# Instruction order taken from the text in place of a scheduler's, with alpha loaded a chunk sooner and the folds and first splits moved

## Chip, cores and metric

One core of one Trainium2 chip. The metric is the device time of one execution in microseconds (us); lower is better. Every time below is in us unless something else is said. Fast runs alone are compared: an execution over 1.5% above the fastest of the same kernel counts as slow.

## The reference, cut to what matters

```python
# q, k, v, alpha: (4, 8, 768, 48) fp32
for t in range(768):                                   # gated linear recurrence
    state = alpha[:, :, t, :, None] * state + einsum('bhd,bhe->bhde', k[:, :, t], v[:, :, t])
    y[:, :, t] = einsum('bhd,bhde->bhe', q[:, :, t], state)
x = y.transpose(0, 2, 1, 3).reshape(3072, 384)         # fp32
out = (((x @ w1) * (x @ w2)) @ w3) @ w_out             # weights float64: 384x1024, 1024x1024, 1024x384
```

## The kernel before

The work falls into three phases, and TensorE (matmul) has to do with all of them:

1. **Recurrence**: 24 chunks of 128 tokens. Per chunk: the running sum of log alpha (`decays`), transposes of q and k, scores, masked attention (`attend`). Its x goes to device memory and comes back transposed, three chunks at a time, as a "token group"; the first gates of groups 0 to 4 are worked in between, from chunk 5, 9, 13, 17 and 21 on.
2. **Gate phase**: the remaining products `x @ w1`, `x @ w2`, each split into three fp32r products (`exact`), and between them eight **folds**, which multiply a row block of w3 into w_out.
3. **Output phase**: 24 projections.

Beside that, VectorE and ScalarE convert float64 weights, bit by bit, into fp32 (`to_fp32`). Each conversion is cut into steps by `yield`, and the text says where a step stands. Before the change a scheduler then moved instructions; the text was only its input.

```python
def to_fp32(dst, *srcs):
    ...                                                     # load raw
    yield
    nc.scalar.activation(rest, low, AF.Copy, scale=2.0 ** -52)                              # L189
    nc.vector.tensor_scalar(top, high, ...)                                                # L190
    nc.vector.tensor_scalar(power, high, 20, 0x7FF, ...)       # exponent, shifted          # L193
    nc.scalar.activation(power, power, AF.Relu, scale=2.0 ** 23, bias=rebias)              # L194
    yield
    nc.vector.scalar_tensor_tensor(mant, top, 2.0 ** -20, rest, ...)                       # L196
    nc.vector.scalar_tensor_tensor(power, high, 0x80000000, power, ...)                    # L197
    nc.vector.tensor_mul(to, mant, power.bitcast(FP32))                                    # L199
    yield
...
def attend(n):
    ...
    for i in range(2):
        nc.scalar.copy(st["x", n][:, :, i], y[i])                                          # L352
    ...
    for half in range(2):
        nc.scalar.dma_start(out=to[half, ...], in_=x[ds(DP * half, D)])    # x to memory    # L358

def load_x(g, queue=nc.sync):
    st["xT", g] = xp.tile([C, KM, TG], FP32, tag="xT", name="xT")
    queue.dma_start(out=st["xT", g], in_=xd[g]...)                                         # L363

def split_x(g, i):
    ...
    nc.scalar.activation(t[:, 0], x, ...)                                                  # L369
    nc.vector.tensor_sub(t[:, 1], x, ...)                                                  # L370
    nc.vector.scalar_tensor_tensor(t[:, 2], ...)                                           # L371

def exact(to, w, x, scale):
    p1, p2 = two of eight PSUM banks
    ... matmuls into p1                                                                    # L380
    nc.scalar.activation(t, p1, AF.Copy, scale=...)            # frees p1                   # L382
    ... matmuls into p2                                                                    # L384
    nc.vector.scalar_tensor_tensor(to, p2, -scale, t, ...)     # frees p2                   # L385
...
for n in range(N):                                             # recurrence
    load_v(n + AHEAD - 1); load_a(n + 5); load_kq(n + AHEAD)
    scores(n)
    if n - 1 in begin:                                         # begin = 4, 8, 12, 16, 20
        split_x(g, 0); fill.extend(gates)
    ...
    early = n < 7
    convert(1, 2 if n == 0 else 3)                             # one step of a conversion
    run(n - 1 not in begin)                                    # half a gate
    advance(n); outer(n)
    if early:
        convert(1)
    transposed(n + 1); decayed(n + 2); logs(n + 4)
    if n in begin:
        load_x(begin[n][0], nc.scalar)
    convert(early and n > 2)
    run(1)
    decays(n + 3); load_ends(n + 2)
    convert(early or n % 3 == 0)
    attend(n)
    run(n - 1 in begin)
```

## Time and profile before

| | before |
|---|---|
| median | 508.95 (508.44 to 510.96, 3 runs) |
| span of the profiled run | 506.3 |
| TensorE busy | 476.6 (94%) |
| first gate starts, last `attend` starts, first projection starts | 56.32, 212.7, 402.68 |

The windows view cuts the span at those three points. Columns: window, its length, then for TensorE, its weight loads, VectorE, ScalarE and GpSimd the busy time with the number of instructions, then the granted TensorE clock, the share of the DMA engines and GB/s.

```profile
0.00:56.30 56.30, 35.95 (x392) 26.11 (x392) 34.37 (x64) 31.01 (x63) 4.65 (x25) 0.91 1.04 198
56.30:212.70 156.40, 150.65 (x1584) 128.20 (x1584) 121.36 (x209) 93.77 (x204) 11.54 (x18) 0.97 0.83 179
212.70:402.70 190.00, 190.00 (x1023) 172.56 (x1020) 146.81 (x277) 90.57 (x166) 0.00 (x0) 1.00 0.39 126
```

Subtract busy from length to read it: TensorE idles for 20.4 before the first gate, 5.8 in the rest of the recurrence, and for nothing in the gate phase, where it has full clock and no gap in 190. VectorE (146.8 of 190) and ScalarE (90.6) have room there. That is a phase in which an order of instructions can only lose.

### The profile page before, as it was taken

To read this page: it belongs to the slowest core of one execution; us is meant where nothing else is said; L and a number is where in the kernel's file an instruction comes from. 1 tells how busy PE (TensorE), PEld (TensorE's weight loads), DVE (VectorE), ACT (ScalarE), POOL (GpSimd) and SP (SyncE) were. 2 spreads that over 40 slices of the span, in tenths; PEclk is the share of its full clock that TensorE was granted. 3 is DMA by queue.
4 is the path that set the end of the run, shared out by engine and by line. 5 is a ranking of instruction groups with operands and counts; after the bars stand their busy time and mean duration, and the time that the engine had idled before them with its cause. 6 is when DMAs were issued, how large, how long until landed. Compare 5 with 4: busy or idle time off the path is not lost.

```text
span 506.3 us, 9496 instructions
## 1 busy us (share of the span) xinstructions
PE 476.6 (94%) x3568; PEld 426.5 (84%) x3568; DVE 371.6 (73%) x620; ACT 250.7 (50%) x479; POOL 16.2 (3%) x43
## 2 busy tenths in 40 slices
PE   3878499999799999999999999999999999999997
PEld 2666388887688888899999988898889899999996
DVE  2777797999777667599999987877434597777771
ACT  3664664867487544365555545454223433333330
POOL 2000002200110000000000000000000000000000
PEclk9979699999899999999999999999999999999999
DMA  9989999999976733165665443321100776655511
GB/s 173 181 216 228 216 215 241 222 225 231 227 173 161 159 80 105 56 178 174 193 193 173 171 159 102 126 88 49 46 33 31 197 231 185 178 174 176 178 54 47
DMA packets 168734, 79.08 MB, mean 156 GB/s; under 512 B 112856, under 2 KB 162544, under 8 KB 168688
## 3 DMA queue, kind: packets, MB, share of 16 engines
q1 hardware_dynamic: 147184, 70.73, 55.3%
q10 hardware_dynamic: 21504, 7.75, 6.7%
q8 instruction: 28, 0.46, 0.4%
q14 instruction: 18, 0.15, 0.1%
HBM read 56.40 MB, written 22.06 MB: 155 GB/s over the span
## 4 chain that ended last, share of the span: by engine, by line
PE 73%; DVE 1%; issue 0%; DVEq 0%
PE bank L380 37%; PE bank L384 18%; PE bank L429 8%; PE bank L348 2%; PE bank L326 2%; PE bank L287 2%; PE bank L423 1%; PE bank L345 1%; PE bank L298 1%; PE bank L256 1%; DVE x L371 0%; DVE x L370 0%; DVE o L385 0%; DVEq L385 0%
## 5 line engine op out<-in xcount | busy, mean ns | idle before, releaser
L380 PE MATMUL bank<-x,w 128*128 128x384 f32 x768 | 162.8, 346 | 10.3 <-ACT x L369 8.0
L380 PEld LDWEIGHTS bank<-x,w 128*128 128x128 f32 x768 | 133.4, 189 | 16.6 <-ACT x L369 8.4
L382 ACT ACTIVATE t<-bank 128x384 f32<-128x384 f32 x152 | 74.4, 491 | 131.8 <-PE bank L380 103.0
L385 DVE SCALAR_TENSOR_TENSOR r<-bank,t 128x384 f32<-128x384 f32 x128 | 69.6, 554 | 49.6 <-ACT t L382 38.3
L384 PE MATMUL bank<-x,w 128*128 128x384 f32 x384 | 88.3, 337 | 1.3 <-DVE x L371 1.3
L384 PEld LDWEIGHTS bank<-x,w 128*128 128x128 f32 x384 | 68.6, 189 | 2.6 <-PE bank L380 1.4
L380 PE MATMUL bank<-w3o,ab 128*128 128x384 f32 x384 | 70.4, 334 | 0.0
L380 PEld LDWEIGHTS bank<-w3o,ab 128*128 128x128 f32 x384 | 66.9, 188 | 0.0
L429 PE MATMUL bank<-wo,w3T 128*128 128x384 f32 x128 | 42.6, 486 | 0.0
L384 PE MATMUL bank<-w3o,ab 128*128 128x384 f32 x192 | 37.2, 334 | 0.0
L429 PEld LDWEIGHTS bank<-wo,w3T 128*128 128x128 f32 x128 | 24.2, 189 | 14.9
L189 ACT ACTIVATE rest<-raw 128x512 f32<-128x512 uint32 (+1 forms) x36 | 23.3, 650 | 26.1 <-DMA raw<-in_moe_w_dram 23.6
L396 DVE TENSOR_TENSOR ab<-r 128x384 f32<-128x384 f32 x64 | 35.5, 555 | 0.9
L448 DVE TENSOR_TENSOR ab<-abl,ab 128x1024 fp32r<-128x1024 f32 x24 | 29.4, 1224 | 9.1 <-ACT ab L447 9.1
L447 ACT ACTIVATE ab<-abl 128x1024 fp32r<-128x1024 f32 x24 | 25.5, 1062 | 19.9 <-PE bank L384 18.8
L384 PEld LDWEIGHTS bank<-w3o,ab 128*128 128x128 f32 x192 | 33.6, 188 | 0.0
L329 DVE TENSOR_TENSOR ms<-bank,keep 128x512 int32<-128x512 int32 x48 | 31.1, 683 | 2.4 <-PE bank L326 2.4
L326 PE MATMUL bank<-qkT 48*128 48x128 f32 x384 | 28.8, 291 | 4.1 <-ACT qkT L288 4.1
L326 PEld LDWEIGHTS bank<-qkT 48*128 48x128 f32 x384 | 24.1, 193 | 9.6 <-ACT qkT L288 5.9
L287 PE MATMUL bank<-ident,qk 128*128 128x128 f32 x192 | 27.9, 291 | 3.9 <-DVE qk L268 3.9
L288 ACT COPY qkT<-bank 128x512 f32<-128x512 f32 x48 | 25.7, 586 | 10.2 <-PE bank L287 8.8
L268 DVE TENSOR_TENSOR qk<-kq,e 128x768 f32<-128x768 f32 x24 | 22.9, 954 | 10.2 <-ACT e L260 5.7
(65 smaller groups left out, 516.6 us busy)
## 6 DMA issues: line engine op xcount, KB each, us to landing
abd<-ab SPq DMA_DIRECT2D x64, 192.0 KB, 2.6
abl<-abd SPq DMA_DIRECT2D x24, 512.0 KB, 4.5
raw<-in_moe_w_dram SPq DMA_DIRECT2D x16, 512.0 KB, 4.4
raw<-in_moe_w_dram SPq DMA_DIRECT2D x24, 256.0 KB, 4.7
ac<-in_alpha_dram SPq DMA_DIRECT2D x24, 192.0 KB, 5.5
kq<-in_k_dram SPq DMA_DIRECT2D x24, 192.0 KB, 5.1
kq<-in_q_dram SPq DMA_DIRECT2D x24, 192.0 KB, 4.9
v<-in_v_dram SPq DMA_DIRECT2D x24, 192.0 KB, 4.7
```

The costliest lines, as they stand in the source:

```text
L287: nc.tensor.transpose(tp[:, ds(j * C, C)], qk[:, i, 2 * j:2 * j + 2, :], ident)
L288: nc.scalar.copy(qkT[:, i], tp.rearrange("p (j c) -> p j c", j=NP))
L326: nc.tensor.matmul(sc[i][:, j, :], qkT[r, 0, j, :], qkT[r, 1, j, :], start=True, stop=True)
L329: nc.vector.tensor_tensor(ms[:, i].bitcast(I32), sc[i].bitcast(I32), keep_bc, op=ALU.bitwise_and)
L380: nc.tensor.matmul(p1, w[part][i], x[part][i], start=(part == i == 0), stop=(part == 1 and i == n - 1))
L382: nc.scalar.activation(t, p1, AF.Copy, scale=(1.0 + 1.0 / P) * scale)
L384: nc.tensor.matmul(p2, w[2][i], x[2][i], start=(i == 0), stop=(i == n - 1))
L385: nc.vector.scalar_tensor_tensor(to, p2, -scale, t, op0=ALU.mult, op1=ALU.add)
L396: nc.vector.tensor_mul(ab, *r)
L429: nc.tensor.matmul(po, w3T[:, j, :], wo[:, j, :], start=(j == 0), stop=(j == KF - 1))
L447: nc.scalar.activation(t[:, 0], ab, AF.Copy, scale=1.0 - 2.0 ** -13)
L448: nc.vector.tensor_sub(t[:, 1], ab, t[:, 0].bitcast(FP32))
```

## The change

The intent is to take the order of instructions on every engine from the text (`manual_schedule`) and to move the text so that this order is a good one: alpha a chunk sooner, a fold in the loop ahead of the conversion of that gate, two first splits of the output phase between the last gates, and other rates of conversion. In full:

```diff
     nc = tc.nc
+    ctx.enter_context(tc.manual_schedule())
...
     def split_ab(n):
-        if n >= N:
+        if ("abl", n) not in st:
             return
...
     load_a(4)
+    load_a(5)
...
         load_v(n + AHEAD - 1)
-        load_a(n + 5)
+        load_a(n + 6)
...
         for _ in x:                       # one gate of the gate phase
             pass
-        owed += 2.7 if folds or folded else 1.2
-        convert(int(owed))
-        owed -= int(owed)
+        owed += 3.0 if folds or folded else 1.3
         if folded < KF:
             ...                           # one step of a fold
...
                 load_ab(n)
+            first = i
+        elif i - first in (1, 3):
+            split_ab(i - first >> 1)
+        convert(int(owed))
+        owed -= int(owed)
     store_ab()
-    split_ab(0)
-    split_ab(1)
+    for n in range(2):
+        split_ab(n)
```

## The prediction

> **What bounds the kernel now.** I read the page first (busy shares, then the 40 slices), then the waits of TensorE, then the timeline around each of its gaps. All times are microseconds.
>
> ```profile
> PE 476.6 (94%) x3568; PEld 426.5 (84%) x3568; DVE 371.6 (73%) x620; ACT 250.7 (50%) x479; POOL 16.2 (3%) x43
> PE   3878499999799999999999999999999999999997
> PEclk9979699999899999999999999999999999999999
> DMA  9989999999976733165665443321100776655511
> ```
>
> TensorE is busy for 94% of 506.3. Its gaps lie in the first eleven slices (to 139 us) and in the last. From 132 us to 502 the chain of waits is TensorE and nothing else, so no reordering can gain there; it can only open gaps. The whole idle time is 506.3 - 476.6 = 29.7, and some 10 of it is start (first alpha, first transposes) and end (last store). **At most about 20 us, 4%, is to be had**, all before 132 us. DMA is full up to slice 12 (150 us).
>
> TensorE's own waits say what the early gaps are:
>
> ```profile
> PE bank L380 <- ACT x L369: 8.0, 2, 6.3
> PE bank L253 <- ACT la L238: 5.6, 2, 4.4
> PE bank L326 <- ACT qkT L288: 4.1, 4, 2.8
> ...
> PE bank L380 <- DVE x L370: 2.3, 2, 1.5
> ```
>
> (total, times, longest.) The first gate of a token group waits for the split of its x (L369, L370, L371); one scores stage waits for the transposed q and k (L288).
>
> **What the change does to the order.** I compared the two programs engine by engine. TensorE's order is the same through the whole recurrence (chunks 0 to 23); only the folds move by a gate later on. What changes is ScalarE, VectorE and the queues: before, a scheduler put conversions and x loads early or late; after, each stands where the text has it. "TensorE: Matmul & The Clock Gate", section "Architectural detail", calls ScalarE and VectorE strict FIFO: so an instruction that waits for a transfer holds up all behind it. The trace agrees: the copies L288 below ran only after L189 had got its data at 30.16. So I go through the places where a text-order wait stands before something TensorE needs.
>
> **Part 1, first weight conversions.** Timeline of before, chunk 2 to 5:
>
> ```profile
> 30.16 0.69 ACT L189 ACTIVATE rest<-raw 128x512 f32<-128x512 uint32 x1 [2.58 <-DMA raw<-in_moe_w_dram]
> ...
> 32.31 1.05 ACT L288 COPY qkT<-bank 128x512 f32<-128x512 f32 x2
> ...
> 33.41 2.08 PE L326 MATMUL bank<-qkT 48*128 48x128 f32 x16 [2.79 <-ACT qkT L288]
> ...
> 42.46 0.39 ACTq L363 DMA_DIRECT2D xT<-xd  x1
> ...
> 55.10 1.17 ACT L369 ACTIVATE x<-xT 128x1152 fp32r<-128x1152 f32 x1
> ...
> 56.32 1.33 PE L380 MATMUL bank<-x,w 128*128 128x384 f32 x3 [6.27 <-ACT x L369]
> ```
>
> The second block of weights lands at 30.16. Before, its L189 stood behind the copies for scores of chunk 2 (those scores ran at 25.22). In text order it stands in front of them, and one alpha load (192 KB, about 0.9 us at the 220 GB/s of these slices) is now ahead of the block in the queue: landing about 31.1, then L190 and L193 (0.8), L194 (0.7), L288 twice (1.1): scores of chunk 2 at about 33.7 in place of 25.2. The chunk after an idle stretch took 7.8 in before (33.41 to 41.23), the next ones 5.3 of work, so chunk 5's transposes end at about 55 in place of 50.0. Half of the loss vanishes there, because before waits then anyway, to 56.32.
>
> What lets before wait is alpha of chunk 8 (L238 at 52.09, after 4.28 idle): **alpha a chunk sooner takes that wait away**. But it isn't the last obstacle any more: the load of x, which the scheduler had issued at 42.46, stands in the text behind chunk 8's logarithm, so it goes out at about 52. Its 576 KB need some 5.5 (the 512 KB loads of the page take 4.4 to 4.5 to land, with queues less full), then L369 1.2: first gate at about 59, +2.7, less the 0.8 that L370 no longer waits. **+1.9.**
>
> **Part 2, the other four x loads.** Groups 1 to 4 start after chunks 8, 12, 16 and 20. Before, group 2:
>
> ```profile
> 120.85 0.59 PE L256 MATMUL bank<-la,sums 128*128 128x384 f32 x2
> ...
> 126.31 1.17 ACT L369 ACTIVATE x<-xT 128x1152 fp32r<-128x1152 f32 x1
> ...
> 127.53 0.79 PE L380 MATMUL bank<-x,w 128*128 128x384 f32 x3 [1.70 <-ACT x L369]
> ```
>
> After, the load stands behind L242, which has one buffer and so waits for L256 of the chunk before it. So it goes out 0.6 after L256; lands about 5.3 later; L369 takes 1.2: 7.1. TensorE has, between L256 and the gate, attend 1.8, scores 1.1, outer 0.7, transposes 1.0: 4.5. **Gap 2.6, then 0.9 for L370 and 0.7 for L371 (1.35 each, less the 0.5 of three matmuls): 4.2.** The 3.8 of group 2 in before (1.70 + 1.51 + 0.57) was followed by a half clock from 131.2 to 135, which cost about 1.4 more. "TensorE: Matmul & The Clock Gate", "The HAM clock gate", says that about 3.4 us of idle window halve the clock and as much work restores it; the trace agrees roughly: 0.50 at 34 to 38, at 54 to 62 and at 132 to 135. So 5.6 a group. Group 1 had a 0.7 gap: +4.9. Group 2 had 5.2: +0.4. Group 3 had none: +5.6. Group 4 has no logarithm before its load, which goes out 2 us sooner: +3. **Sum +13.9.**
>
> "DMA: Bandwidth & Descriptors", "Issuing engines are not separate DMA queues", says that both queues share the 16 engines; so the ScalarE-issued load shares with the SyncE loads, which before kept the engines at 1.0 to 1.4 of their time there. For the change speaks that the weight loads are no longer hoisted: after chunk 7 one 512 KB block in three chunks, and no w_out block until the recurrence is over.
>
> **Part 3, folds.** One fold of before (timeline, 338 to 346):
>
> ```profile
> 338.95 5.32 PE L429 MATMUL bank<-wo,w3T 128*128 128x384 f32 x16
> ...
> 344.30 0.49 ACT L432 ACTIVATE w3o<-bank 128x384 fp32r<-128x384 f32 x1 [0.41 <-PE bank L429]
> 344.83 0.56 DVE L433 SCALAR_TENSOR_TENSOR w3o<-w3o,bank 128x384 fp32r<-128x384 f32 x1 [1.84 <-ACT w3o L432]
> ```
>
> After, VectorE's order in every second gate is L433, L434 of fold i, then L196, L197, L199 of the second half of w3 row i+1, and one gate later TensorE transposes that row. Counted from the end of L429 (344.27): L433 starts at +0.56, L434 ends at +1.6, then three operations that start 0.6 apart and last 0.68: +3.5. TensorE finishes the gate between at about +2.9. So it waits about 0.65 in each of 7 folds: **+4.6**. That the folds stand "a gate behind their weights" keeps this from being four times as much. Before, both halves of a row were finished ahead of L433, and TensorE had no gap. Ahead of the folds, VectorE was 97% busy from 220 to 280 us; in order, a gate with a conversion has about 2.7 of VectorE work, and 1.2 of waiting for L194 and the next L382 in four gates out of ten: about 3.2 against 3.12 of TensorE, over 20 gates, most of it taken up by the eight banks: +0.5.
>
> **Part 4, output phase.** The two first splits stand between the last gates, so their 1.06 on ScalarE and 2.4 on VectorE lie beside gates of 3.12; before, the scheduler put them there too, and the chain shows no gap at 402 us. Then 24 projections of 4.16, TensorE alone. **0.**
>
> **Sum.** 1.9 + 13.9 + 4.6 + 0.5 = 20.9 on 509: 530.
>
> **Rivals.**
> (a) *The order is the cure.* The 7.1 of idle and the half clock around the first gate go away because alpha no longer comes late, and in-order conversions no longer steal ScalarE in front of the splits (group 2's L369 at 126.31 stood behind a conversion's L189 and L194, 1.4 together). All early gaps but the start closed would give some 495; one or two of them closed 503. For it: 17.8 of waits for alpha in before, and constants in the diff (1.3 and 3.0 per gate) that look as if tuned. Against it: x load and first block stand late by the text, and neither wait depends on alpha.
> (b) *Transfers get quicker.* With no hoisted loads the engines are less full, x lands in 4 instead of 5.5, and the gaps stay short enough for the full clock: then group 1 costs +2, group 2 nothing, group 3 +2.7, group 4 +1, first gate +0.5, folds +4: about 518.
> (c) *Nothing to see.* TensorE has two gates' worth of banks to run ahead, and hides everything but the gap at the start: 507 to 511. Against it: it can't run ahead in the recurrence, where scores, transposes and the gate stand in one fixed order on it.
> (d) *Worse than my sum.* The x load goes out behind a semaphore of a SyncE load that landed late, or the weight block lands at 33 rather than 31: 535 to 540.
>
> **Range and chances.** My own sum says 530, rival (b) 518; both are slower by about 2 to 4%. I move the number down, to 523, because several terms are estimates of landing times of which the trace before shows no instance, and because the constants look as if someone had found the new order good. Eight times in ten: 506 to 535. Faster by over 2% needs under 498.8, which asks for nearly every gap to close: 0.06. Within 2% is up to 519.1, rival (c) and the better half of (b): 0.34. Slower: 0.60.
>
> **What would show each step right or wrong.** Part 1: ScalarE's L189 of the second block (one line lower in the new text) waits for its load before the copies of chunk 2, with a TensorE gap of 7 to 9 us near 26 to 34; the wait of L238 for alpha falls from 17.8 to under 10; the first gate starts at 57 to 61. Part 2: gaps of 3 to 5 us ahead of the first gate in groups 1, 2 and 3, with a half clock behind them; group 4 smaller. Part 3: seven gaps of 0.4 to 1 us ahead of the transposes of w3, in VectorE's name. Part 4: no TensorE gap at the turn to the output phase. I am wrong if TensorE's idle time is 30 us or less: then the x loads or the first block landed well before their users. A total near 500 with no gap ahead of the later groups would mean that rival (a) holds.

## More of the kernel before

One line of the waits view of all engines will matter (engine, tile and line that waits, what it waits for, total, number of times, longest):

```profile
ACT power L194 <- DVE power L193: 7.1, 11, 1.0
```

ScalarE's exponent step of a conversion hardly ever waits for VectorE's shift.

In the changed kernel every line number is one higher than before (L194 becomes L195); some experiments add lines: in e5 the exponent step is L201, a gate's matmuls L390 and the copy that frees a bank L392; in e9 the split of x is L372; in e10 to e14 the exponent step is L201, a gate's matmuls L392 and L396, the transposes of a w3 row L435.

## The result

The changed kernel took **547.1** (median of 4 runs, 543.4 to 548.0), the kernel before 509.3 beside it (508.4 to 511.0). Ratio 1.073, 95% interval 1.066 to 1.080: **7.3% slower**, outside the predicted range of 506 to 535. Ratios in this document are the mean time of one kernel's fast runs over that of the other's of the same rounds, so not quite the ratio of the medians quoted. The profiled run of the changed kernel (span 541.6) was its fastest; the three others were 547 to 548. Two more runs, 543.8 and 550.5, aren't in that median but are in the ratio.

The page of the changed kernel, shares and clock by slice:

```profile
PE 492.6 (91%) x3568; PEld 434.4 (80%) x3568; DVE 378.4 (70%) x620; ACT 245.5 (45%) x479; POOL 18.0 (3%) x43
...
PEclk9979699799799899999999999999899999999999
```

The same number of matmuls, but TensorE is busy for 16.0 more and idle for 19.3 more (541.6 - 492.6 = 49.0, against 29.7). Busy rises because slices with a half clock have come in: there are now four under 0.8 (the 3rd, 5th, 8th and 11th), where before there were two (the 3rd and 5th). The windows view, cut at the same three events:

```profile
0.00:60.00 60.00, 40.20 (x393) 28.96 (x393) 35.02 (x64) 31.03 (x64) 5.08 (x25) 0.91 1.15 210
60.00:231.50 171.50, 156.91 (x1582) 131.91 (x1582) 119.19 (x199) 90.24 (x197) 12.90 (x18) 0.93 0.64 143
231.50:438.00 206.50, 195.49 (x1023) 173.85 (x1020) 156.88 (x288) 89.02 (x173) 0.00 (x0) 0.99 0.40 128
```

So +3.7 up to the first gate, +15.1 in the rest of the recurrence, **+16.5 in the gate phase**, and nothing in the output phase (103.6 both times). Milestones of TensorE beside the steps of the prediction:

| TensorE starts | before | after | lag | what that step added | predicted |
|---|---|---|---|---|---|
| first gate | 56.32 | 59.98 | 3.7 | +3.7 | +1.9 |
| scores of chunk 9 | 90.1 | 93.1 | 3.0 | | |
| scores of chunk 10 (behind group 1) | 99.2 | 109.5 | 10.3 | +7.3 | +4.9 |
| scores of chunks 13, 14 (around group 2) | 123.0, 137.2 | 132.3, 148.3 | 9.3, 11.1 | +1.8 | +0.4 |
| scores of chunks 17, 18 (around group 3) | 161.3, 168.7 | 172.5, 185.3 | 11.2, 16.6 | +5.4 | +5.6 |
| scores of chunks 21, 22 (around group 4) | 192.2, 199.9 | 208.8, 218.8 | 16.6, 18.9 | +2.3 | +3 |
| last attend | 212.7 | 231.5 | 18.8 | | 15.8 |
| first projection | 402.68 | 437.96 | 35.3 | +16.5 | +5.1 |

TensorE's own waits in the changed kernel:

```profile
PE bank L381 <- ACT x L370: 16.9, 5, 5.3
...
PE bank L424 <- DVE w L200: 4.9, 2, 2.5
PE bank L327 <- ACT qkT L289: 4.9, 2, 4.6
PE bank L381 <- ACT t L383: 3.4, 5, 0.8
PE bank L381 <- DVE r L386: 2.7, 3, 1.2
```

The first is the wait for the split of x, five groups, up from 8.0. The second is the transposes of a w3 row, the third the copies of chunk 2. The last two are new in the gate phase: TensorE waits for a PSUM bank that ScalarE (L383) or VectorE (L386) has not yet read.

**How a group waits for its x.** Timeline of the changed kernel, group 1:

```profile
91.67 0.45 ACTq L364 DMA_DIRECT2D xT<-xd  x1
...
97.17 1.70 ACTq L359 DMA_DIRECT2D xd<-x  x2
98.91 1.16 ACT L370 ACTIVATE x<-xT 128x1152 fp32r<-128x1152 f32 x1 [4.95 <-DMA kq<-in_q_dram]
...
100.13 0.79 PE L381 MATMUL bank<-x,w 128*128 128x384 f32 x3 [4.23 <-ACT x L370]
```

The load of x goes out at 91.67. ScalarE's own queue then holds the two stores of chunk 8's x. They are issued only at 97.17, and the split L370 stands behind them: 98.91. TensorE idles for 4.23. In this trace the 356 transfers of the two queues use eight semaphores (44 or 45 transfers on each), and the instruction that issues a transfer first waits until the last transfer on its semaphore has landed. The first of the two stores has the semaphore of the load of x, so it goes out when x has landed, 5.5 after 91.67: up to there the split would have had to wait too. What the stores add is the 1.74 from 97.17 to 98.91, and most of that is a wait as well: asked from 98 on, the view shows the second store at 98.55, on the semaphore of the load of q issued at 91.81. "Perfetto Trace Analysis", section "DMA Instruction — HWDGE (DVE, Sync)", says that the profiled window of such an instruction opens when its semaphores are satisfied, so that the wait before isn't in the record. The trace agrees: each store's own record lasts 0.31, and the 3.2 between the copies of that chunk (they end at 93.96) and 97.17 show only within the idle time of 4.95 of the next compute instruction. After such a gap the clock halves: in windows of 2 and 3 us it is 0.50 from 102 to 107.

**How the gate phase loses.** Timeline of the changed kernel, one gate:

```profile
256.57 0.35 DVE L194 TENSOR_SCALAR power<-raw 128x384 uint32<-128x384 uint32 x1
...
256.96 0.62 ACT L195 ACTIVATE power<-power,rebias 128x384 uint32<-128x384 uint32 x1 [4.20 <-DVE power L194]
...
257.48 0.85 ACT L383 ACTIVATE t<-bank 128x384 f32<-128x384 f32 x2
...
258.00 1.34 PE L381 MATMUL bank<-x,w 128*128 128x384 f32 x6 [0.23 <-ACT t L383]
```

ScalarE reaches the exponent step L195 early and then stands still for 4.20, since VectorE does the shift (L194) only after the two splits of x and the products of its gate. The copies L383, which free banks that TensorE has filled, stand behind L195 on ScalarE. VectorE's next products (L386) need those copies, and the next shift stands behind L386. Two strictly ordered engines wait for each other once a conversion. The waits view gives its size, against 7.1 in 11 times before:

```profile
ACT power L195 <- DVE power L194: 85.9, 32, 5.7
```

Ahead of the folds the 50 double products of 1.56 (78.0) took 85.4, from 232.6 to 318.0: 5.3 in gaps of 0.2 to 1.2, the rest in matmuls that overlap less on both sides of a gap (1.34 above, 1.20 in the usual case). The folds lost 9 more: 2.7 and 4.2 in two cycles where VectorE also has a split of x in front of the last product of a w3 row (waits of 2.5 and 2.4; behind the second the clock was 0.66 for 5 us), 1.1 in the first fold, and the rest in five cycles 0.2 longer each.

### The profile page after: what moved, and what is told of

Its sections match the earlier page's. It is cut to its first block, busy times and chain, and to the rows that moved or that the text cites. A ratio compares the mean times of both kernels' runs of the same rounds, so it can differ in the third digit from the quotient of the medians.

```text
span 541.6 us, 9466 instructions
## 1 busy us (share of the span) xinstructions
PE 492.6 (91%) x3568; PEld 434.4 (80%) x3568; DVE 378.4 (70%) x620; ACT 245.5 (45%) x479; POOL 18.0 (3%) x43
## 4 chain that ended last, share of the span: by engine, by line
PE 43%; DVE 10%; issue 4%; ACT 2%; DMA 1%; DVEq 0%; SPq 0%; ACTq 0%
PE bank L381 23%; PE bank L385 11%; PE bank L430 6%; DVE r L386 3%; DVE x L372 2%; DVE ab L397 2%; PE bank L424 1%; ACT x L370 1%; DVE power L198 1%; DVE mant L197 1%; DMA abd<-ab 1%; DVE power L194 1%; PE bank L349 1%; DVE w L200 1%; ACT t L383 0%
## 5 line engine op out<-in xcount | busy, mean ns | idle before, releaser
L381 PE MATMUL bank<-x,w 128*128 128x384 f32 x768 | 167.5, 353 | 24.9 <-ACT x L370 16.9
L381 PEld LDWEIGHTS bank<-x,w 128*128 128x128 f32 x768 | 134.9, 192 | 35.6 <-ACT x L370 18.0
L383 ACT ACTIVATE t<-bank 128x384 f32<-128x384 f32 x152 | 70.9, 485 | 94.9 <-PE bank L381 74.6
L386 DVE SCALAR_TENSOR_TENSOR r<-bank,t 128x384 f32<-128x384 f32 x128 | 67.4, 553 | 47.5 <-ACT t L383 43.0
L385 PE MATMUL bank<-x,w 128*128 128x384 f32 x384 | 90.5, 344 | 1.1 <-DVE x L372 1.0
L385 PEld LDWEIGHTS bank<-x,w 128*128 128x128 f32 x384 | 70.0, 193 | 3.1 <-DVE x L372 1.2
L195 ACT ACTIVATE power<-power,rebias 128x512 uint32<-128x512 uint32 (+1 forms) x36 | 25.1, 698 | 86.1 <-DVE power L194 85.9
L330 DVE TENSOR_TENSOR ms<-bank,keep 128x512 int32<-128x512 int32 x48 | 30.9, 685 | 10.6 <-PE bank L327 10.5
L327 PE MATMUL bank<-qkT 48*128 48x128 f32 x384 | 29.7, 298 | 4.9 <-ACT qkT L289 4.9
L448 ACT ACTIVATE ab<-abl 128x1024 fp32r<-128x1024 f32 x24 | 25.4, 1060 | 18.8 <-PE bank L385 18.8
L371 DVE TENSOR_TENSOR x<-xT,x 128x1152 fp32r<-128x1152 f32 x12 | 16.3, 1357 | 20.4 <-ACT x L370 20.4
```

The source lines that it names most:

```text
L327: nc.tensor.matmul(sc[i][:, j, :], qkT[r, 0, j, :], qkT[r, 1, j, :], start=True, stop=True)
L330: nc.vector.tensor_tensor(ms[:, i].bitcast(I32), sc[i].bitcast(I32), keep_bc, op=ALU.bitwise_and)
L381: nc.tensor.matmul(p1, w[part][i], x[part][i], start=(part == i == 0), stop=(part == 1 and i == n - 1))
L383: nc.scalar.activation(t, p1, AF.Copy, scale=(1.0 + 1.0 / P) * scale)
L385: nc.tensor.matmul(p2, w[2][i], x[2][i], start=(i == 0), stop=(i == n - 1))
L386: nc.vector.scalar_tensor_tensor(to, p2, -scale, t, op0=ALU.mult, op1=ALU.add)
```

## The experiments

The kernel before ran beside each (medians 508.1, 510.5, 508.5 and 508.9 in the four sets), so ratios to it are compared. The changed kernel stands at 1.073.

### Is it the order, or the edits?

**e1**: the changed kernel with the scheduler left on.

```diff
-    ctx.enter_context(tc.manual_schedule())
```

> The kernel after, but with the scheduler allowed to reorder again (the other parts of the change kept). Theory A (waits in text order are the whole loss): within 1% of before, 505 to 513, and the recurrence ends near 214 us. Rival B (the later folds, the higher conversion rates or the sooner alpha load cost something by themselves): 515 to 530.

Measured 509.5, ratio 1.002 (0.997 to 1.008). The last attend starts at 209.6 and the first projection at 400.35.

**e2**: the kernel before with that line alone.

> The kernel before with nothing changed but the order of the text on all engines. Theory A: slower than after, 550 to 570: alpha late again (some 5 us in chunks 4 to 8) and each w3 transpose waits in the gate of its own conversion (8 folds by 1 to 2 us), and the first splits stand alone in front of the output phase (some 4 us). Rival B (the rest of the change is what costs): 520 to 535.

Measured 567.3, ratio 1.118 (1.112 to 1.124). So the loss is wholly that of the order: with a scheduler the edits cost and gain nothing, and in the order of the text they are worth 4% (1.118 against 1.073). Where they gain is plain from the milestones: e2's recurrence ended at 229.3, 2 *sooner* than in the changed kernel, but its gate phase took 230.5 against 206.5. TensorE's waits of e2:

```profile
PE bank L424 <- DVE w L200: 20.7, 8, 3.8
```

This is the wait for a w3 row in all eight folds. With the edits it is 4.9. The prediction had given this to the folds standing a gate behind their weights ("keeps this from being four times as much"); no run separates that edit from the changed rates of conversion.

### The gate phase: does the exponent step hold up the banks?

**e5**: the changed kernel; in the gate phase, ScalarE's exponent step is emitted behind the two PSUM copies of the next gate. VectorE's order is left as it is.

```diff
-        nc.scalar.activation(power, power, AF.Relu, scale=2.0 ** 23, bias=rebias)
+        held.append(lambda: nc.scalar.activation(power, power, AF.Relu, ...))
+        if not hold:                # hold is True in the gate phase
+            flush()
         yield
+        flush()
...
         for _ in x:                 # one gate
             pass
+        flush()
```

> The kernel after, but in the gate phase each conversion's exponent step on ScalarE (which waits for VectorE's shift) is placed behind the next gate's two PSUM copies. Theory D (ScalarE and VectorE run in lockstep: ScalarE's 86 us of waiting for the shift stands in front of the copies TensorE's banks wait for): the 7.4 us lost ahead of the folds fall to under 2 and the folds' 9 us to about 6, total 535 to 539. Rival E (VectorE has too much work there, since no output-weight block is converted in the recurrence any more): 545 to 549, with VectorE over 95% busy from 260 to 340 us.

Measured 533.6, ratio 1.052 (1.048 to 1.057). The gate phase, from the last attend at 233.9 to the first projection at 425.39, takes **191.5 in place of 206.5** (before: 190.0). TensorE has no gap after 217. Timeline of e5, a gate at the same time of the program:

```profile
257.64 0.35 DVE L200 TENSOR_SCALAR power<-raw 128x384 uint32<-128x384 uint32 x1
...
258.03 0.62 ACT L201 ACTIVATE power<-power,rebias 128x384 uint32<-128x384 uint32 x1 [0.58 <-DVE power L200]
...
258.39 1.20 PE L390 MATMUL bank<-x,w 128*128 128x384 f32 x6
...
258.56 0.49 ACT L392 ACTIVATE t<-bank 128x384 f32<-128x384 f32 x1
```

ScalarE now comes to the exponent step when the shift is about done (0.58 of idle in place of 4.20) and TensorE runs on. In the gate phase the wait of ScalarE for the shift falls from 70.9 in 24 places to 16.7 in 17. VectorE's and ScalarE's busy time in the phase hardly changed (155.2 and 92.1, from 156.9 and 89.0), so it was not VectorE's load (rival E: over 95% busy from 260 to 340; it was 83%, and 90% in e5) but the place of one ScalarE instruction. The fold gaps at the splits vanished with it, which I had not expected; no run separates them.

### The x loads: sooner, and ahead of what?

**e3**: the load of x at the start of its chunk's text, ahead of the conversions and the logarithm.

```diff
+        if n in begin:
+            load_x(begin[n][0], nc.scalar)
         convert(1, 2 if n == 0 else 3)
...
-        if n in begin:
-            load_x(begin[n][0], nc.scalar)
         convert(early and n > 2)
```

> The kernel after with the five loads of x issued at the start of their chunk, in front of its conversion and its gate pieces, not behind the logarithm. Theory A (the split waits for a load issued too late): TensorE's waits for the split's first part fall from 16.9 us to under 5, lags of the recurrence fall by 10 to 14 us in all, total 531 to 537. Rival C (the transfers are slow in themselves, or the split is held up by the stores in front of it on the same queue): under 4 us gained, 543 or more.

Measured 537.6, ratio 1.059 (1.053 to 1.065). The recurrence ends at 223.0 in place of 231.5, and the gaps of groups 1 to 4 shrink to about 0.6 to 2.2. But the first gate comes 3.7 *later*, at 63.66. So Theory A is right in kind and was too hopeful in size: 8.5 gained by the end of the recurrence, not 10 to 14, and 11.4 of waits left for the split's first part, 8.1 of them at the first gate.

**e6**: the load one chunk sooner still, ahead of that chunk's attend.

```diff
-        if n in begin:
-            load_x(begin[n][0], nc.scalar)
         ...
         convert(early or n % 3 == 0)
+        if n + 1 in begin:
+            load_x(begin[n + 1][0], nc.scalar)
         attend(n)
```

> The changed kernel with each group's x load issued in the chunk before the one in whose text it stood, just ahead of that chunk's attend copies. My theory (the x load stands too late in ScalarE's text): the TensorE gaps ahead of the first gate of groups 1, 2 and 4 fall from 4 to 5 us to under 1, without the half clock behind them, the first gate is not later than 60.0, the recurrence ends at 217 to 222 in place of 231.5 and the total falls to 531 to 538; better than with the load at the start of its own chunk (537.6), where it was caught by the stores. Rival (transfers are slow anyway, or the wait goes to conversions): gaps of 3 us or more stay and the total is over 541.

Measured 539.8, ratio 1.057 (1.050 to 1.064). My expectation failed: the recurrence ended at 228.8 and the first gate came at 65.4. A load that is sooner still took 8.2 from the stretch between the first gate and the last attend (163.4 for 171.5; e3 took 12.2) and lost 5.5 ahead of it, and group 2 kept a gap of 3.0. Timeline of e6:

```profile
49.72 0.41 ACTq L364 DMA_DIRECT2D xT<-xd  x1
...
61.93 2.25 ACTq L359 DMA_DIRECT2D xd<-x  x2
64.22 1.16 ACT L370 ACTIVATE x<-xT 128x1152 fp32r<-128x1152 f32 x1 [2.32 <-DMA raw<-in_moe_w_dram]
```

x was long there (ScalarE's own wait for the semaphore of that load had ended by 57.23), and the split ran at 64.22, behind the two stores of chunk 4. The releaser that the profile names is a weight load: it was for that load's semaphore that the second store waited, from 62.26 to 63.85. So the theory needed its second half: not only the load's place counts, but which transfers ScalarE has to issue between.

**e9**: e6, with the split put between the copies of that chunk's attend and its stores.

```diff
         x = st.pop(("x", n)).rearrange("p j i t -> p (j i) t")
+        if n in begin:
+            split_x(begin[n][0], 0)
         ...
         for half in range(2):
             nc.scalar.dma_start(...)            # stores of x
...
         if n - 1 in begin:
             g, tiles = begin[n - 1]
-            split_x(g, 0)
```

> The changed kernel with x loads issued a chunk sooner (as in the run before of that kind, 539.8) and, besides, the split of x put ahead of the stores of that chunk's x on ScalarE's queue (in that run the split stood behind two stores, and the second store waited up to 3 us for a semaphore that earlier loads still used). My theory (a DMA issue that waits holds up ScalarE): the gaps ahead of the first gates of groups 1 to 4 vanish or stay under 0.7, the first gate comes at 56 to 60 in place of 65.4, the recurrence ends at 214 to 220 in place of 228.8, total 525 to 532. Rival (x lands late, the stores are innocent): the first gate stays at 63 or later and the total is over 534.

Measured 531.6, ratio 1.047 (1.043 to 1.052). The recurrence ends at 218.6: 10 less than e6, by a move of three instructions over two stores (on VectorE, two of the three also moved over the masks of the next chunk's scores; that isn't tested apart). The gaps of groups 1, 3 and 4 are under 0.7, as expected; group 2 still has 1.9 and 0.6, and the first gate came at 62.0, not at 56 to 60, so there the stores were only part of it.

**e11**: the changed kernel with the stores of x and the small transfers of row ends issued on GpSimd's queue.

```diff
-            nc.scalar.dma_start(out=to[half, ...], in_=x[...])
+            nc.gpsimd.dma_start(out=to[half, ...], in_=x[...])
         # likewise the three stores to ends and the load of decs
```

> The changed kernel with the small transfers and the x stores issued on GpSimd's queue in place of ScalarE's; the load of x stays on ScalarE's. If ScalarE's stalls at DMA issues cost the early part: the split of x follows the landing of its load without the 1 to 3 us of stores in front, the recurrence ends 5 to 9 sooner (222 to 226), total 538 to 542. If the load's own place is what matters: under 2 us of gain, 545 or more. If GpSimd's own issuing is slow, the stores land later, and the total rises above 549.

Measured 540.4, ratio 1.061 (1.056 to 1.067): the time is in the first range, but the milestones are not. The profiled recurrence ended at 229.1, not at 222 to 226, and profile against profile the gain is only 2.2, since the profile of the changed kernel is of its fastest run. TensorE's waits for the split did fall, from 16.9 to 10.5. A gain of some 1% is likely; what it comes from inside isn't shown by this run, for the trace shows that the move changed three things. ScalarE no longer issues the stores. On GpSimd's queue they use eight semaphores of their own, so that they and the loads no longer wait for each other's landing. And the same bytes move in 152,815 packets where it had been 168,733.

### The first weight block, and alpha

**e4**: the conversion steps of chunk 1 moved behind the copies of chunk 2.

```diff
-        convert(1, 2 if n == 0 else 3)
+        if n != 1:
+            convert(2 if n == 2 else 1, 2 if n == 0 else 3)
...
-        if early:
-            convert(1)
+        if early and n != 1:
+            convert(2 if n == 2 else 1)
...
-        convert(early or n % 3 == 0)
+        convert(n != 1 and (early or n % 3 == 0))
         attend(n)
+        convert(n == 1)
```

> The changed kernel with the steps of the second weight block put behind the copies of chunk 2 (they stood in front, and held ScalarE until 30.2). My theory: scores of chunk 2 start at 25 to 27 in place of 32.8 and those of chunk 3 at 33 to 35 in place of 40.8, but the first gate, which waits for the load of x issued behind chunk 8's logarithm, moves by less than 3 from 60.0; total 0 to 3 less than the changed kernel's 547 (544 to 547). Rival: the 7 us of lag that arises there is carried through to the end, then 540 or less.

Measured 549.3, ratio 1.075 (1.070 to 1.079): no gain, much as my theory had it (544 to 547), but not for its reason. Scores of chunk 2 did come at 28.0 (32.8), yet those of chunk 3 stayed at 40.5:

```profile
40.51 2.08 PE L327 MATMUL bank<-qkT 48*128 48x128 f32 x16 [5.42 <-ACT qkT L289]
```

The steps that I had saved up stood in a heap in front of the copies of chunk 3, and the same wait went over to it. The first gate came even 4 later (64.2), where I had expected less than 3.

**e8**: the changed kernel with alpha at its old place.

```diff
-    load_a(5)
-        load_a(n + 6)
+        load_a(n + 5)
```

> The changed kernel with alpha loaded at its old place (one chunk later). My theory: alpha a chunk sooner gives nothing in the order of the text, as something else (x load, weight block) is the last to come: 543 to 549. Rival (a) of the prediction (alpha is what the early part waits for): 552 or more. A third possibility, from the copy of the old text in text order, whose recurrence ended 2 us earlier than the changed kernel's: alpha sooner costs 2, then 543 to 545.

Measured 545.2, ratio 1.069 (1.064 to 1.075); the changed kernel's 1.073 (1.066 to 1.080) overlaps it. Alpha sooner is worth nothing here: rival (a) of the prediction is out. So is the third possibility, since this recurrence ended at 232.4, not sooner than 231.5.

### Putting the parts together

**e7**: e4, e5 and e6 in one kernel.

> All three repairs in the order of the text: second weight block later, x loads a chunk sooner, exponent step of a conversion behind the next gate's copies in the gate phase. If the three losses are separate, as my theory has it: the gate phase is 190 to 193 long, the recurrence ends at 212 to 220, and the total is 545 - 14 - 10 to 15 = 513 to 523. If they share one cause (say, lag that is only passed on), it stays above 525. To beat the kernel before (508) the recurrence would have to end before 210.

Measured 522.1 (median of three fast runs; the slow one took 529.6), ratio 1.023 (1.018 to 1.028). Gate phase 191.5, as in e5; recurrence 224.8, later than expected, though 6.7 sooner than in the changed kernel, which is more than e4 (5.4 later) and e6 (2.7 sooner) give apart; what they do together isn't explained. The gate phase and the recurrence are separate losses.

**e10**: e9 and e5, and the first two conversion steps of chunk 1 simply left out there (all later steps move back by two).

```diff
-        convert(1, 2 if n == 0 else 3)
+        convert(n != 1, 2 if n == 0 else 3)
...
-        if early:
+        if early and n != 1:
             convert(1)
```

> The same, with the exponent step behind the next gate's copies in the gate phase and the first two conversion steps of chunk 1 left out (so that the second weight block is waited for behind the copies of chunk 2). Sum of the parts: 525 to 532 less 15 less 0 to 3 = 508 to 517, that is, level with the kernel before or up to 2% slower. Under 506 would mean that text order with these placements beats the scheduler.

Measured 517.6, ratio 1.018 (1.015 to 1.021): just above the expected range. The recurrence ended at 214.9 and the first gate came at 55.9, both sooner than in e9 (218.6, 62.0); but the gate phase was back at 198.2.

**e12**: e10 with the transfers of e11 on GpSimd's queue.

> All placements of the fourfold repair, and the small transfers and stores on GpSimd's queue as well. If the stalls at ScalarE's issues are still there in the fourfold repair, this is 3 to 8 below it; if the split's new place has already dealt with them, within 2 of it.

Measured 512.6, ratio 1.009 (1.006 to 1.011), 5 less than e10: the gain is the one expected if ScalarE's stalls at issues were still there, and it lies in the recurrence alone (the gate phase takes 198.2 in both). As with e11, the freed queue, the separate semaphores and the fewer packets aren't told apart. The recurrence ended at 209.1, ahead of the 212.7 of before. TensorE's waits of e12:

```profile
PE bank L355 <- POOL T L327: 7.6, 2, 6.0
...
PE bank L435 <- DVE w L209: 6.7, 7, 1.0
```

The second line is a surprise and a lesson: seven waits of about 0.95 for the last product of a w3 row, **exactly the shape that the prediction had given to the folds** (seven of 0.65), and which the changed kernel did not show. In e10 and e12 two steps less in chunk 1 shift every later step by two, so a different step of a conversion stands beside each part of a fold. If that is it, two steps given back anywhere before the gate phase take it away.

**e13**: e12 with the two steps given back in chunks 22 and 23.

```diff
-        convert(early or n % 3 == 0)
+        convert(early or n % 3 == 0 or n > 21)
```

> The fourfold repair with stores on GpSimd's queue (512.6), in which the two conversion steps left out in chunk 1 had shifted every later step, so that the folds ran in cycles of 13.46 with a wait of 0.95 for the last product of a w3 row in each of seven. Here the two steps are given back in chunks 22 and 23. If the waits in the folds depend only on which conversion step stands beside which part of a fold (my theory): cycle 12.5, seven waits gone, total 512.6 - 7 x 0.95 = 505 to 507, level with or just below the kernel before. Rival (the fold cycle follows from VectorE's load as a whole, which is unchanged): 511 to 514 again.

Measured **505.6** (505.3 to 505.9, 6 runs), ratio 0.993 (0.990 to 0.995): 0.7% under the kernel before, the best of both and of all runs. The folds run in cycles of 12.5 in place of 13.5, and the seven waits are gone from TensorE's list. Its windows:

```profile
54.60:207.90 153.30, 148.46 (x1583) 126.21 (x1583) 121.08 (x204) 89.58 (x199) 46.75 (x83) 0.99 0.72 168
207.90:399.40 191.50, 191.50 (x1022) 172.44 (x1019) 156.36 (x290) 91.70 (x173) 1.16 (x2) 1.00 0.43 138
```

Set beside the changed kernel's windows, all of the loss is back: 153.3 for 171.5 with a clock of 0.99 for 0.93, and 191.5 for 206.5 without idle time. VectorE's load in the gate phase is the same (156.4, against 156.9 in e12 and in the changed kernel). The fold term depends on the phase of the steps, not on the load. ScalarE still waits for the shift in the gate phase, 17.3 in 17 places, and it costs TensorE nothing.

**e14**: e13 with the third step of chunk 1 left out as well and given back in chunk 19, so that the copies of chunk 1's attend don't wait for the second weight block.

```diff
-        convert(early or n % 3 == 0 or n > 21)
+        convert(n != 1 and (early or n % 3 == 0) or n in (19, 22, 23))
```

> The same with the third conversion step of chunk 1 left out too and given back in chunk 19, so that the copies of chunk 1's attend no longer stand behind the wait for the second weight block on ScalarE (in the run before, GpSimd's stores and its scaling of the state stood behind those copies, and TensorE waited 6.0 for the state). If that wait is what is left of the loss at the start: attend of chunk 2 starts at 30 to 33 in place of 36.9, the first gate 0 to 3 sooner, total 500 to 505. Rival (the wait only moves on to the copies of chunk 3): within 2 of the run beside it.

Measured 508.3, ratio 0.998 (0.996 to 1.001): slower than e13. The first part came out as expected (attend of chunk 2 at 31.8 in place of 36.2, first gate at 51.0 in place of 54.6), and then the bill came. Timeline of e14:

```profile
72.05 1.33 PE L392 MATMUL bank<-x,w 128*128 128x384 f32 x3 [2.44 <-ACT w L217]
```

With a step less in hand the second pair of gates waits for its weights; with 1.1 before it and 0.9 behind it, TensorE is busy for 3.9 of the 8 us from 66 to 74, and the clock is 0.64 from 70 to 72 and 0.50 from 72 to 80. The wait for the weights moved, and the half clock came with it.

## Why the prediction was wrong

Direction and place were right: slower, with nothing to gain after 132 us, and the loss in the recurrence and the gate phase. The size was not: +20.9 by its own sum (and +14 after the hand had moved it), +35.3 between the profiles.

- **The step that failed** is the last of Part 3, "ahead of the folds": "about 3.2 against 3.12 of TensorE, over 20 gates, most of it taken up by the eight banks: +0.5". It measured +7.4 there, and e5 shows the mechanism: the prediction had seen that ScalarE's L194 and L382 stand in each other's way, but took it for a load of VectorE that a buffer of banks would absorb. It is a lock: while ScalarE waits for the shift it frees no bank, so the banks, which were to take up the wait, fill up because of it. All in all e5 gave back 15.0 of the 16.5 of the gate phase.
- **Folds, +4.6.** It measured +9, but not by the seven small waits: an ordinary fold cycle was only 0.2 longer. Two cycles with a split of x in VectorE's text lost 6.9 of it. The predicted mechanism does exist, at 0.95 each, in e10 and e12, and e13 shows that the phase of the conversion steps decides whether it appears. In the changed kernel that phase was right: the loss in the folds was double the estimate and came from another cause, so that the term was there at all is luck.
- **x loads, +13.9**, measured as 15.1 between the first gate and the last attend (15.9 by the reckoning of the next point). Right in the mechanism and near in size: the estimate of 5.3 to 5.5 for the landing holds (91.67 to 97.17), and so does the half clock. "TensorE: Matmul & The Clock Gate", "The HAM clock gate", was a sound guide: gaps of 4 to 5 brought 0.50. What was missed is the pair of stores ahead of the split, some 1.7 in group 1; rival (d) had named a semaphore of another load as the possible surprise, for the load of x; e6 and e9 show it at the stores.
- **First block and first gate, +1.9**, measured as +3.7. Scores of chunk 2 came at 32.8 (33.7 predicted), the second block landed by 30.22 (31.1 predicted), and half of the 7.6 was absorbed, as predicted. The first gate came at 60.0 (59 predicted), and the 0.8 that it was to win back behind that is there too: its third part starts 2.7 after its first, in the kernel before 3.5. By the prediction's own reckoning that makes +2.8. The gap ahead of the scores of chunk 2 was 4.6, not 7 to 9.
- **Alpha.** That its wait would go was right (17.8 in the kernel before, 2.3 in the changed one), and that this would give nothing as well. But alpha a chunk sooner is not what took it away: with alpha at its old place, in text order, it is 3.0 (e8) and 2.4 (e2).
- **Output phase, 0.** Right.
- **One reading.** "DMA is full up to slice 12" is a slice too long: the twelfth digit is 7. Nothing rests on it.
- **The choice to move the sum from 530 to 523** "because the constants look as if someone had found the new order good" was a guess about people, not a reading of the profile. e2 shows what the constants were good for: with the rest of the edits they are 4% better than the old text in the same order, and still 7% worse than the scheduler.

What stays open: the gap of 1.9 that group 2 keeps in e9, why e11 alone shows so little in its milestones, which of three things gave e12 its gain, and which part of e5's gain in the folds is due to the lock and which to what came ahead.

## What to carry to other kernels

In an order taken from the text, ask of each cross-engine wait not how long it is but what stands behind it: an instruction that waits for a partner must not stand in front of one that frees a buffer the partner, or TensorE, lives on. Count the issue of a transfer as such an instruction too, since it may wait for a semaphore that a stranger's load still holds; put it behind the compute that someone needs, or on a queue with nothing to do. And when steps are left out at one place, every later step is shifted against its surroundings: give them back before the next phase, or measure that phase again.

## What the Trainium skill lacked or had wrong

- "DMA: Bandwidth & Descriptors", section "Issuing engines are not separate DMA queues", says that issuing from several engines "will only save the time on the sequencer it takes to initiate the DMA, which is usually small relative to the DMA itself". It lacks what an issue costs that has to wait for a semaphore with compute behind it: in e6 the second of two stores on ScalarE's queue stood for 1.6 (62.26 to 63.85) until a weight load had landed, with the split of x behind it. With the small transfers issued on GpSimd's queue the time fell from 517.6 to 512.6 (e10, e12), though not only the issuing engine changed there.
- No page has the lock of two strictly ordered engines over PSUM banks: in the gate phase 70.9 of waits of ScalarE for VectorE in 24 places cost 15.0 of time (206.5 to 191.5, e5), at hardly changed load of both engines. "TensorE: Matmul & The Clock Gate", section "Architectural detail", has the strict order of ScalarE and VectorE but not what it does to buffers.
- "TensorE: Matmul & The Clock Gate", section "The HAM clock gate", names one idle window of about 3.4 as what halves the clock, and a later section of that page says that frequent short idles do so too, without their lengths. Gaps of 4.2 did (0.50 from 102 to 107 in the changed kernel), but so did shorter ones close together: in e14 gaps of 1.1 and 2.4 within 6 us (0.50 from 72 to 80), in the changed kernel's group 3 gaps of 2.0, 0.6 and 0.5 within 5 us (0.50 from 180 to 182). Gaps of 0.3, 0.6 and 0.6 in its group 4 did not (1.00 from 210 to 216).
